# Six stages a batch in place of eight: two columns of 506 or 508 tokens, and w_out's parts reloaded in every stage

## The chip, the cores and the metric

The kernel runs on one core of one Trainium2 chip. The metric is device time in microseconds, the median of several runs. Before the change: 2146.05 us, median of 3 runs (2146.03 to 2146.26).

## The reference

Channel attention followed by two layers of an MLP with squared relu. B = 2, N = 6080 tokens in each batch, C = 256, F = 2048; all float32, the weights float64.

```
qn = q / (norm(q, axis=1) + 1e-6);  kn = k / (norm(k, axis=1) + 1e-6)
a  = softmax(kn^T qn / tau)                 # 256 x 256 for each batch, sums over 6080 tokens
x  = v @ a                                  # [2 * 6080, 256]
x  = (relu(x @ w_in1)^2) @ w_out1           # first layer
out = (relu(x @ w_in2)^2) @ w_out2          # second layer
```

## The kernel before

The program is written in one order by hand (a manual schedule); each engine takes its own instructions from it in that order, and so does SP, which issues all DMAs.

**Attention.** Batch 0's 256 x 256 matrix of scores is made first, from whole tiles, with all engines at it. Its softmax `a` is multiplied into w_in1 (`fuse`, L225, matmuls of 512 columns), so that v needs no matmul of its own. Batch 1's scores are made later, beside the products of batch 0: 24 pieces of 256 tokens. For each piece and each of its two halves `b1_hi` (a cast on ACT), `b1_lo` (a subtraction on DVE), `b1_square` (ACT), `b1_sum` (DVE) and `b1_scores` (six matmuls of 256 columns, L159, into PSUM bank m3) run, and then `b1_add` (DVE, from m3).

**Precision.** Each float32 operand is split into a high and a low float32r part, and a product is three matmuls: high by high, high by low, low by high. The high part is a copy on ACT, the low part a subtraction on DVE.

**Stages, pairs, slots.** The tokens are worked off in stages of two columns of W = 380 tokens: 8 stages for a batch and a layer, 32 in all. In a stage the 16 rows of 128 of F go by pairs: 8 pairs Q. For a pair, h = w_in^T x is made in 7 products of blocks in place of 8 (Winograd's form of Strassen's): `product(Q, k)`, k = 0 to 6, three matmuls each (L806). One product is one slot. Its results go through PSUM banks m0 or m1 (product 3 of the pair before, then 0, 2 and 4), m2 (1 and 5) and m3 (6).

Behind each product `after(Q, k)` issues the elementwise work: the copies u1, u2, u3 out of PSUM, the adds into r (L780), the relu, and for each of the two halves of the pair `square` (on ACT: gh, the high part of the square, L811, and the square itself in r, L812). `lows` (DVE: gl = r - gh) follows one pair later. `relu` goes to ACT or DVE by the table `act_relu`. The y matmuls with w_out (`y_stream`, L870, 24 for a pair, into four banks of their own) run some ten slots behind, 3 or 4 behind each product. At the end of a stage `y_done` copies y out of PSUM and stores it, in the first layer to DRAM (x2d), in the second to the output.

**Background work.** Everything else is put into slots by the table `TIMES` through `at(Q, t, fn)`: slot t after the start of pair Q, a half for behind `after`. So go the right operands of the next stage (`Right`: the load of x, four sums on DVE, seven high parts on ACT, seven low parts on DVE, most of them in the last slots of a stage), the left operands of w_in (`left_steps`), batch 1's pieces (one every two pairs) and its softmax, the first layer's w_out (`conv_task`), and during batch 1 the second layer's weights, whose parts wait in DRAM (wad, wod).

**w_out.** The parts of w_out's eight blocks stay in eight tiles wo0 to wo7 (512 KB each) for a whole layer; `get_out` (L750) loads the second layer's once, in the last stage of the first.

**Tiles.** r0, r1, gh0, gh1, gl0 and gl1 have two buffers each, of 2W words; yo0 and yo1 one of 2W words, stored once a stage.

Of the kernel before, what the change touches and what calls it, by code (L numbers as in the profile page):

```python
# [20 lines left out]
W = 380  # L21
NS = N // (2 * W)
KQ = 7
Y_FIRST = 3
# The order of the work beside the products. Background steps: when they are emitted, in slots (one product each, KQ to a
# pair of rows of f), half a slot for behind the slot's own work. "loads": batch 0's pieces of q and k (p), blocks of weights
# (w) and x; "start": what goes between the pieces and the softmax's steps: the conversion of weights (a, s, m, h, l: as a
# float32 by its steps, its high and its low part) and the first right operands (t: sums, x: high and y: low parts). "rows":
# how many rows of a piece's squares are left to the tensor engine; "act_relu": up to which pair of rows the scalar engine
# does a relu.  # L30
# [21 lines left out]
    "wo": -3,  # L52
    "rows": (1, 1, 1, 1, 1, 2, 1, 1, 1, 1, 1, 2, 1, 1),
    "act_relu": (0, 0, 98, 18),
# [18 lines left out]
def tile_attention_mlp_mlp(  # L73
# [19 lines left out]
    wts = ctx.enter_context(tc.tile_pool(name="wts", bufs=1))  # L93
# [7 lines left out]
    def f32(ap):  # L101
        return ap.bitcast(F32)
# [18 lines left out]
    # A float64 weight as two float32r parts. Its upper word, read as a float32, grows with the weight's size; times 2^16  # L121
    # and held within float32's exponents, its bits shifted by 3 are those of the weight as a float32.
# [192 lines left out]
    with tc.manual_schedule():  # L315
        wa, wo, right = {}, {}, {}
        wop = [ctx.enter_context(tc.tile_pool(name="wop0", bufs=1))]
# [8 lines left out]
        with tc.tile_pool(name="att0", bufs=1) as a0:  # L326
# [76 lines left out]
            # the weights' conversion: one after another, each in steps that the engines' queues take apart  # L403
# [93 lines left out]
            # the first pair of rows' left operands, and what the second's come from, where w_out's last part goes later  # L497
# [16 lines left out]
        wop.append(ctx.enter_context(tc.tile_pool(name="wop1", bufs=1, reuse_waits="tile")))  # L514
# [430 lines left out]
```

## Time and profile before

| | |
|---|---|
| runs | 2146.03, 2146.05, 2146.26 us; median 2146.05 |
| profiled execution, span from first to last instruction | 2140.9 us |
| instructions | 30939 |
| TensorE matmul busy | 2123.4 us (99%), 12264 matmuls |
| DVE busy | 1649.5 us (77%) |
| ACT busy | 1507.8 us (70%) |
| DMA | 128.08 MB, mean 60 GB/s |

The page gives the span of the profiled execution, from its first to its last instruction; its own device time is not listed, and the runs, taken without the profiler, are 5.1 us longer than the span. Busy time of an engine is the union of its instructions' times. Matmuls are pipelined: one is reported as longer than the interval to the next, so the interval between starts, not the reported length, says how fast they go.

### The profile page before, as it was taken

The numbers are of one execution on the slowest core, as the hardware profiler recorded it, in microseconds if no ns is written. First come the engines' busy times: TensorE is split into PE (matmuls) and PEld (weight loads), VectorE is DVE, ScalarE is ACT, GpSimd is POOL, SyncE is SP. The second block draws the span as 40 slices with busy tenths as digits, with TensorE's granted clock in tenths as the row PEclk, the third lists the DMA queues.
The fourth block names the chain that finished last, engine by engine and source line by source line (L and its number), as shares of the span: only waits on it lengthen the run. The fifth ranks groups of instructions, "written<-read, shape, count | busy, mean of one in ns | idle before, by whom it ended". The sixth has DMA issues, their size and how long they took to land.

```text
span 2140.9 us, 30939 instructions
## 1 busy us (share of the span) xinstructions
PE 2123.4 (99%) x12264; PEld 2107.0 (98%) x12264; DVE 1649.5 (77%) x3110; ACT 1507.8 (70%) x2473; POOL 0.7 (0%) x6
## 2 busy tenths in 40 slices
PE   9899999999999999999999999999999999999999
PEld 8799999999999999999999999999999999999999
DVE  7987788878877878788797777777777777777775
ACT  5688778778777777767676666666666666666665
POOL 0000000000000000000000000000000000000000
PEclk9999999999999999999999999999999999999999
DMA  9511111111121212211162000000000000000000
GB/s 347 197 49 45 59 63 66 38 51 57 50 74 45 94 50 76 77 50 69 45 240 100 30 30 30 15 16 30 30 30 30 30 15 16 30 30 30 30 16 15
DMA packets 41857, 128.08 MB, mean 60 GB/s; under 512 B 4784, under 2 KB 5168, under 8 KB 41712
## 3 DMA queue, kind: packets, MB, share of 16 engines
q1 hardware_dynamic: 41712, 126.11, 16.4%
q8 instruction: 96, 1.57, 0.3%
q14 instruction: 49, 0.40, 0.1%
HBM read 85.46 MB, written 40.63 MB: 59 GB/s over the span
## 4 chain that ended last, share of the span: by engine, by line
PE 98%; ACT 1%; DVE 0%; DMA 0%; SPq 0%; issue 0%
PE ps_y L870 50%; PE ps_m L806 43%; PE ps_m L371 2%; PE ps_m L159 2%; PE ps_m L165 1%; PE ps_m L230 0%; PE ps_m L231 0%; PE ps_m L232 0%; DMA araw<-in_q 0%; ACT gh L811 0%; ACT r L812 0%; ACT r L784 0%; SPq L127 0%; DVE x L105 0%; ACT L174 0%
## 5 line engine op out<-in xcount | busy, mean ns | idle before, releaser
L806 PE MATMUL ps_m<-x,wa 128*128 128x380 f32 x5376 | 1221.6, 335 | 6.7 <-DVE u L818 2.2
L870 PE MATMUL ps_y<-gh,wo 128*128 128x380 f32 x4096 | 1164.3, 335 | 0.0
L806 PEld LDWEIGHTS ps_m<-x,wa 128*128 128x128 f32 x5376 | 960.2, 188 | 9.9 <-DVE u L818 2.6
L870 PEld LDWEIGHTS ps_y<-gh,wo 128*128 128x128 f32 x4096 | 746.9, 188 | 0.8
L780 DVE TENSOR_TENSOR r<-u,ps_m 128x380 f32<-128x380 f32 x768 | 421.0, 548 | 398.9 <-PE ps_m L806 208.5
L870 PE MATMUL ps_y<-gl,wo 128*128 128x380 f32 x2048 | 689.3, 337 | 0.0
L811 ACT ACTIVATE gh<-r 128x760 fp32r<-128x760 f32 x512 | 426.3, 833 | 229.1 <-DVE r L786 226.0
L105 DVE TENSOR_TENSOR gl<-r,gh 128x760 fp32r<-128x760 f32 x512 | 483.0, 943 | 6.1 <-ACT r L812 4.8
L812 ACT ACTIVATE r<-r 128x760 f32<-128x760 f32 x512 | 430.5, 841 | 16.3
L870 PEld LDWEIGHTS ps_y<-gl,wo 128*128 128x128 f32 x2048 | 384.6, 188 | 0.5 <-DVE gl L105 0.3
L786 DVE TENSOR_SCALAR r<-r 128x380 f32<-128x380 f32 x652 | 233.3, 358 | 22.4
L836 ACT ACTIVATE r<-ps_m 128x380 f32<-128x380 f32 x256 | 124.8, 488 | 118.2 <-PE ps_m L806 115.9
L832 ACT COPY u<-ps_m 128x380 f32<-128x380 f32 x256 | 122.1, 477 | 106.9 <-PE ps_m L806 105.0
L818 DVE COPY u<-ps_m 128x380 f32<-128x380 f32 x256 | 140.9, 551 | 10.6
L826 ACT COPY u<-ps_m 128x380 f32<-128x380 f32 x256 | 121.3, 474 | 29.8 <-PE ps_m L806 28.3
L784 ACT ACTIVATE r<-r 128x380 f32<-128x380 f32 x116 | 60.5, 522 | 79.9 <-DVE r L780 78.9
L105 DVE TENSOR_TENSOR x<-xt,x 128x380 fp32r<-128x380 f32 x128 | 67.7, 548 | 4.2 <-ACT x L310 1.7
L310 ACT CAST x<-xt 128x380 fp32r<-128x380 f32 x128 | 61.2, 503 | 0.0
L105 DVE TENSOR_TENSOR x<-xraw,x 128x380 fp32r<-128x380 f32 x96 | 52.5, 547 | 0.0
L371 PE MATMUL ps_m<-araw 128*128 128x256 f32 (+1 forms) x192 | 48.0, 402 | 3.4 <-DMA araw<-in_q 3.4
L310 ACT CAST x<-xraw 128x380 fp32r<-128x380 f32 x96 | 48.4, 504 | 0.0
L852 DVE COPY yo<-ps_y 128x380 f32<-128x380 f32 x64 | 35.3, 552 | 13.6 <-PE ps_y L870 13.6
(117 smaller groups left out, 757.1 us busy)
## 6 DMA issues: line engine op xcount, KB each, us to landing
xraw<-in_vT SPq DMA_DIRECT2D x32, 380.0 KB, 3.7
x2d<-yo SPq DMA_DIRECT2D x32, 380.0 KB, 2.3
xraw<-x2d SPq DMA_DIRECT2D x32, 380.0 KB, 3.5
out_T<-yo SPq DMA_DIRECT2D x32, 380.0 KB, 2.3
raw<-in_w_in SPq DMA_DIRECT2D x16, 512.0 KB, 5.0
raw<-in_w_out SPq DMA_DIRECT2D x16, 512.0 KB, 3.9
wad<-unit SPq DMA_DIRECT2D x8, 896.0 KB, 3.6
wa<-wad SPq DMA_DIRECT2D x8, 896.0 KB, 5.4
```

The costliest lines, as they stand in the source:

```text
L105: nc.vector.tensor_tensor(out=out, in0=a, in1=b, op=ALU.subtract)
L310: nc.scalar.copy(self.hi[m], self.operand(m))
L780: nc.vector.tensor_tensor(out=out, in0=a, in1=b, op=op)
L786: nc.vector.tensor_scalar_max(r, r, 0.0)
L806: nc.tensor.matmul(ps, a, b, start=(n == 0 and first), stop=(n == 2), skip_group_check=True)
L811: nc.scalar.square(gh, r)
L812: nc.scalar.square(r, r)
L818: nc.vector.tensor_copy(m["u2"], m[Q, 3])
L826: nc.scalar.copy(u3, m[Q, 3])
L832: nc.scalar.copy(m[Q + 1, "u1"], m[Q + 1, 3])
L836: nc.scalar.activation(m["r", 0][:, 1, :], m[Q, 3], AF.Relu)
L870: nc.tensor.matmul(y[c, n], a, b[:, f, :], start=(p == 0 and f == 0 and x == 0), stop=(p == NQ - 1 and f == 1 and x == 2), skip_group_chec ...
```

## The change

The stages become wider and fewer: the two columns of a stage have 508, 508, 506, 506, 506 and 506 tokens, six stages for a batch and a layer, 24 in all. Each pair has the same matmuls as before, with that many columns.

The wider tiles take the place of w_out in memory. w_out has four tiles in turn in place of eight. In the first stage each block's parts are stored to DRAM once they are made (`stash_out`, w2d), and from the second stage on every stage loads all eight blocks again (`get_out`), each issued at slot 4 of the pair before its own. r and gl have three buffers each for both halves, gh four. gl's tile is taken in `lows` and not in `square`. yo0 and yo1 have one column, and each is stored by itself, two stores for each of them in a stage.

The slots of the background work move. Batch 1's pieces come three in four pairs (`b1_at`) in place of one in two, its softmax is closer packed, and the second layer's weights are converted every 10 pairs in place of 16. `act_relu` counts pairs, and is scaled with their number.

```diff
-W = 380
-NS = N // (2 * W)
+WIDTHS = (508, 508, 506, 506, 506, 506)
+NS = len(WIDTHS)
+W = max(WIDTHS)
+STARTS = [2 * sum(WIDTHS[:i]) for i in range(NS)]
...
-    "wo": -3,
+    "wo": -2,
+    "stash": (0.0, 0.5, 1.0),
+    "get_out": 4.0,
-    "act_relu": (0, 0, 98, 18),
+    "act_relu": (0, 0, 74, 14),
...
-    "b1_hi": (3.0, 5.0),
-    "b1_lo": (4.5, 7.0),
-    "b1_square": (5.0, 9.5),
-    "b1_sum": (9.5, 13.0),
-    "b1_scores": (8.5, 9.0),
-    "b1_add": (9.5,),
-    "b1_soft": (0.0, 2.0, 4.5, 8.0, 9.0, 13.0, 16.5, 16.5, 18.0, 24.0, 24.5),
+    "b1_at": (3.0, 12.5, 22.0),
+    "b1_load": -8.0,
+    "b1_hi": (2.0, 3.5),
+    "b1_lo": (3.0, 4.5),
+    "b1_square": (3.5, 6.0),
+    "b1_sum": (6.0, 8.5),
+    "b1_scores": (5.5, 6.0),
+    "b1_add": (6.5,),
+    "b1_soft": (0.0, 1.5, 3.5, 6.5, 7.0, 9.5, 12.0, 11.5, 12.5, 15.5, 16.5),
...
         def out_tile(n):
-            return wop[n // 4].tile([P, 2, 512], F32R, tag=f"wo{n}", name="wo")
+            return wop.tile([P, 2, 512], F32R, tag=f"wo{n % 4}", name="wo")
...
-            ("w1l", 1024, 1), ("u1", W, 2), ("u2", W, 1), ("u3", W, 1), ("r1", 2 * W, 2), ("r0", 2 * W, 2),
-            ("big", 2048, 1), ("gh1", 2 * W, 2), ("gl1", 2 * W, 2), ("gh0", 2 * W, 2), ("gl0", 2 * W, 2),
-            ("yo0", 2 * W, 1), ("yo1", 2 * W, 1),
+            ("w1l", 1024, 1), ("u1", W, 2), ("u2", W, 1), ("u3", W, 1), ("r", 2 * W, 3), ("big", 2048, 1),
+            ("gh", 2 * W, 4), ("gl", 2 * W, 3), ("yo0", W, 1), ("yo1", W, 1),
...
         for n in range(NP1):
-            Q = NQ + 2 * n
-            at(Q - 2, 2, b1_load, n)
+            Q = NQ + (B1_AT[n % 3] + n // 3 * 4 * KQ) / KQ
+            at(Q, TIMES["b1_load"], b1_load, n)
...
+        def stash_out(n):
+            nc.sync.dma_start(w2d[n], f32(wo[n]))
...
+        UNIT_EVERY = 10
         for j in range(4):
-            Q = Q2 + 2 * NQ * j
+            Q = Q2 + UNIT_EVERY * j
...
-        def get_out(n):
+        def get_out(n, src):
             wo[n] = out_tile(n)
-            nc.sync.dma_start(f32(wo[n]), wod[n])
+            nc.sync.dma_start(f32(wo[n]), src[n])
...
+        for s in range(1, 2 * B * NS):
+            for p in range(NQ):
+                at(s * NQ + p - 1, TIMES["get_out"], get_out, p, w2d if s < B * NS else wod)
...
         def lows(Q, n):
-            gh, gl, r = g[Q, n]
+            gh, r = g[Q, n]
+            gl = g[Q, n][1] = work_tile("gl", r.shape, F32R, 3)
             sub(gl, r, f32(gh))
...
+            yo = work_tile(f"yo{c}", [P, w], F32)
+            (nc.scalar.copy if c else nc.vector.tensor_copy)(yo, y[c, n])
+            o = i // NS * N + STARTS[i % NS]
+            dst = x2d[i][c] if layer == 0 else outT[c * P:(c + 1) * P, o:o + 2 * w]
+            nc.sync.dma_start(dst[:, n * w:(n + 1) * w], yo)
```

How this moves instructions is seen in the order in which each engine has them. In these rows the number in a tile's name tells buffers apart, and the brackets name the engines or DMA queues that a row waits for. TensorE before, at the scores of any of batch 1's pieces (ps_m3 is bank m3, big the piece's parts, x and wa the operands of the products):

```order
L806 MATMUL ps_m2_1768<-x_1431,wa_823 128x380 [waits DVE_49]
L806 MATMUL ps_m2_1768<-x_1432,wa_823 128x380
L806 MATMUL ps_m2_1768<-x_1431,wa_823 128x380
L159 MATMUL ps_m3_1773<-big_1714 128x256 [waits DVE_49]
L159 MATMUL ps_m3_1773<-big_1714 128x256 x5
L870 MATMUL ps_y00_1674<-gh0_1663,wo_632 128x380
L870 MATMUL ps_y10_1691<-gh0_1663,wo_632 128x380
L870 MATMUL ps_y10_1691<-gl0_1664,wo_632 128x380
```

The first six scores stand behind product 1, which is in bank m2. TensorE with the change, at the third piece of a group of three (the sixth of all):

```order
L828 MATMUL ps_m3_2272<-x_1239,wa_1249 128x508
L828 MATMUL ps_m3_2272<-x_1240,wa_1249 128x508
L828 MATMUL ps_m3_2272<-x_1239,wa_1249 128x508
L166 MATMUL ps_m3_2282<-big_2228 128x256 [waits DVE_49,Activation_49]
L166 MATMUL ps_m3_2282<-big_2228 128x256 x5
L893 MATMUL ps_y11_1670<-gl_2203,wo_2048 128x508
L893 MATMUL ps_y11_1670<-gh_2164,wo_2048 128x508
L893 MATMUL ps_y00_1691<-gh_2178,wo_2048 128x508
```

They stand behind product 6 now, which is in the same bank m3. DVE with the change at that place; the wait of TensorE above is for the add that reads ps_m3_2272:

```order
L801 TENSOR_TENSOR r_2215<-u2_2188,ps_m2_2198 128x508 [waits PE_49]
L112 TENSOR_TENSOR big_2228<-raw_2083,big_2228 128x2x256 [waits Activation_49]
L112 TENSOR_TENSOR x_2231<-xt_1684,x_2230 128x506
L801 TENSOR_TENSOR r_2249<-u1_2123,ps_m3_2272 128x508 [waits PE_49]
L807 TENSOR_SCALAR r_2249<-r_2249 128x508 [waits DVE_49]
```

Between the add of product 5 and that of product 6 DVE has the low part of the piece's second half and a step of the right operands. ACT before, around the two casts of a piece (big):

```order
L568 CAST big_3000<-raw_2788 128x2x256 [waits DMAHW7_49,DMAHW0_49]
L832 COPY u1_3002<-ps_m1_2996 128x380 [waits PE_49]
L836 ACTIVATE r0_2986<-ps_m0_2906 128x380 [waits PE_49]
L568 CAST big_3000<-raw_2788 128x2x256
L574 ACTIVATE raw_2788<-raw_2788 128x2x256 [waits DVE_49]
L784 ACTIVATE r1_2987<-r1_2987 128x380 [waits DVE_49]
L811 ACTIVATE gh1_3025<-r1_2987 128x760 [waits Activation_49]
L812 ACTIVATE r1_2987<-r1_2987 128x760 [waits Activation_49]
L811 ACTIVATE gh0_3039<-r0_2986 128x760 [waits DVE_49]
L812 ACTIVATE r0_2986<-r0_2986 128x760 [waits Activation_49]
```

And with the change, at the first piece of a group:

```order
L576 CAST big_2365<-raw_2212 128x2x256 [waits DMAHW2_49,DMAHW1_49]
L805 ACTIVATE r_2325<-r_2325 128x506 [waits DVE_49]
L833 ACTIVATE gh_2369<-r_2325 128x1012 [waits Activation_49]
L834 ACTIVATE r_2325<-r_2325 128x1012 [waits Activation_49]
L833 ACTIVATE gh_2383<-r_2351 128x1012 [waits DVE_49]
L834 ACTIVATE r_2351<-r_2351 128x1012 [waits Activation_49]
L576 CAST big_2365<-raw_2212 128x2x256
L582 ACTIVATE raw_2212<-raw_2212 128x2x256
```

The second cast moved from ahead of the four squares to behind them.

## Rows read from the trace of the kernel before

**Rows 1.** The page's chain of work that ended last, by engine and by line.

```profile
PE 98%; ACT 1%; DVE 0%; DMA 0%; SPq 0%; issue 0%
PE ps_y L870 50%; PE ps_m L806 43%; PE ps_m L371 2%; PE ps_m L159 2%; PE ps_m L165 1%; PE ps_m L230 0%; PE ps_m L231 0%; PE ps_m L232 0%; DMA araw<-in_q 0%; ACT gh L811 0%; ACT r L812 0%; ACT r L784 0%; SPq L127 0%; DVE x L105 0%; ACT L174 0%
```

**Rows 2.** The page's groups: TensorE's matmuls (busy us, mean ns, idle before, releaser).

```profile
L806 PE MATMUL ps_m<-x,wa 128*128 128x380 f32 x5376 | 1221.6, 335 | 6.7 <-DVE u L818 2.2
L870 PE MATMUL ps_y<-gh,wo 128*128 128x380 f32 x4096 | 1164.3, 335 | 0.0
...
L870 PE MATMUL ps_y<-gl,wo 128*128 128x380 f32 x2048 | 689.3, 337 | 0.0
```

**Rows 3.** Busy us (instructions) by stretch: PE, PEld, DVE, ACT, POOL; clock, DMA share, GB/s.

```profile
130.00:550.00 420.00, 420.00 (x2515) 420.00 (x2514) 332.50 (x591) 334.91 (x565) 0.00 (x0) 1.00 0.15 50
1080.00:1120.00 40.00, 40.00 (x233) 40.00 (x232) 37.70 (x79) 29.34 (x52) 0.00 (x0) 1.00 0.81 280
1200.00:2000.00 800.00, 800.00 (x4622) 800.00 (x4621) 584.84 (x1088) 522.43 (x832) 0.00 (x0) 1.00 0.07 26
```

**Rows 4.** Timeline of TensorE at 593 us: six fused matmuls (start us, us, instruction).

```profile
593.76 0.39 PE L230 MATMUL ps_m<-w1h,e 128*128 128x512 f32 x1
593.99 0.40 PE L231 MATMUL ps_m<-w1l,e 128*128 128x512 f32 x1
...
595.15 0.51 PE L870 MATMUL ps_y<-gh,wo 128*128 128x380 f32 x2
```

**Rows 5.** Timeline of TensorE at 329 us: two sets of six scores.

```profile
329.41 0.88 PE L159 MATMUL ps_m<-big 128*128 128x256 f32 x6
330.12 0.51 PE L870 MATMUL ps_y<-gh,wo 128*128 128x380 f32 x2
...
331.16 0.88 PE L159 MATMUL ps_m<-big 128*128 128x256 f32 x6
331.88 0.51 PE L870 MATMUL ps_y<-gh,wo 128*128 128x380 f32 x2
```

**Rows 6.** DMA issues: count, KB each, median us from issue to landing.

```profile
x2d<-yo SPq DMA_DIRECT2D x32, 380.0 KB, 2.3
...
wo<-wod SPq DMA_DIRECT2D x8, 512.0 KB, 3.9
```

**Rows 7.** Groups with shapes kept apart, DVE and ACT.

```profile
L780 DVE TENSOR_TENSOR r<-u,ps_m 128x380 f32<-128x380 f32 x768 | 421.0, 548 | 398.9 <-PE ps_m L806 208.5 <-ACT u L826 188.6
...
L598 DVE TENSOR_TENSOR sacc<-sacc,ps_m 128x512 f32<-128x512 f32 x23 | 15.6, 680 | 0.0
...
L812 ACT ACTIVATE r<-r 128x760 f32<-128x760 f32 x512 | 430.5, 841 | 16.3
L811 ACT ACTIVATE gh<-r 128x760 fp32r<-128x760 f32 x512 | 426.3, 833 | 229.1 <-DVE r L786 226.0
...
L784 ACT ACTIVATE r<-r 128x380 f32<-128x380 f32 x116 | 60.5, 522 | 79.9 <-DVE r L780 78.9
...
L568 ACT CAST big<-raw 128x512 fp32r<-128x512 f32 x48 | 29.6, 616 | 0.0
...
L380 ACT ACTIVATE asq<-araw 128x1024 f32<-128x1024 f32 x1 | 1.1, 1056 | 0.9 <-DMA araw<-in_q 0.9
```

**Rows 8.** Timeline at 157 us: four squares on ACT; a subtraction and the next on DVE.

```profile
157.21 0.84 ACT L811 ACTIVATE gh<-r 128x760 fp32r<-128x760 f32 x1
...
160.43 0.46 ACT L852 COPY yo<-ps_y 128x380 f32<-128x380 f32 x1
...
158.15 0.68 DVE L105 TENSOR_TENSOR big<-raw,big 128x512 fp32r<-128x512 f32 x1
158.75 0.55 DVE L818 COPY u<-ps_m 128x380 f32<-128x380 f32 x1
```

**Rows 9.** Timeline: DVE behind TensorE at 1505 us, TensorE behind DVE at 90 us.

```profile
1505.36 0.68 PE L806 MATMUL ps_m<-x,wa 128*128 128x380 f32 x3
1506.08 0.55 DVE L780 TENSOR_TENSOR r<-u,ps_m 128x380 f32<-128x380 f32 x1 [0.82 <-PE ps_m L806]
...
90.39 0.54 DVE L818 COPY u<-ps_m 128x380 f32<-128x380 f32 x1
...
90.99 0.44 PE L806 MATMUL ps_m<-x,wa 128*128 128x380 f32 x1 [2.24 <-DVE u L818]
```

**Rows 10.** The chain in order of time, at the start of the products.

```profile
74.21 1.39 DVE x L105 x3
```

More of the change, by code (lines that the diff above doesn't have):

```diff
@@ L20 @@
 NQ = F // P // 2
-W = 380
-NS = N // (2 * W)
+WIDTHS = (508, 508, 506, 506, 506, 506)
+NS = len(WIDTHS)
+W = max(WIDTHS)
+STARTS = [2 * sum(WIDTHS[:i]) for i in range(NS)]
+assert 2 * sum(WIDTHS) == N
 KQ = 7
@@ L243, in left_tile @@
     def left_tile(p):
-        return wts.tile([P, 2, KQ, P], F32R, tag=f"wa{p}", name="wa")
+        return wts[p // 4].tile([P, 2, KQ, P], F32R, tag=f"wa{p}", name="wa")
     def left_steps(dst, wf, r, sums):
@@ L272, in left_steps @@
         return sums1, hi1, sums2, lo1, hi2, lo2
-    x2d = [dram.tile([CC, P, 2 * W], F32, name=f"x2d{i}") for i in range(B * NS)]
+    x2d = [dram.tile([CC, P, 2 * WIDTHS[i % NS]], F32, name=f"x2d{i}") for i in range(B * NS)]
     class Right:
@@ L290, in x @@
         def x(self, c, n):
-            return self.raw[:, c, n * W:(n + 1) * W]
+            return self.raw[:, c, n * self.w:(n + 1) * self.w]
         def sums(self, n):
             if n == 0:
-                self.t = [xp.tile([P, W], F32, tag=f"xt{i}", name="xt") for i in range(4)]
+                self.t = [xp.tile([P, self.w], F32, tag=f"xt{i}", name="xt") for i in range(4)]
             t, x = self.t, self.x
@@ L307, in split_hi @@
             self.hi[m], self.lo[m] = [
-                xp.tile([P, W], F32R, tag=f"x{t}{m}", name="x", bufs=1 if m < 4 else 2) for t in "hl"
+                xp.tile([P, self.w], F32R, tag=f"x{t}{m}", name="x", bufs=1 if m < 4 else 2) for t in "hl"
             ]
@@ L554, in tile_attention_mlp_mlp @@
         NP1 = -(-N // (2 * P))
+        B1_AT = TIMES["b1_at"]
         def b1_load(n):
@@ L681, in tile_attention_mlp_mlp @@
             fused_tasks(NQ * NS + 2 * j - 4, 1, j)
-        for n in range(len(wo), NQ):
+        w2d = [dram.tile([P, 2, 512], F32, name=f"w2d{p}") for p in range(NQ)]
+        def stash_out(n):
+            nc.sync.dma_start(w2d[n], f32(wo[n]))
+        for n in range(NQ):
+            if n in wo:
+                at(0, TIMES["stash"][n], stash_out, n)
+                continue
             def wo_hi(n=n):
@@ L801, in product @@
             if first:
-                m[Q, k] = bank({1: "m2", 3: a, 6: "m3"}[k])[:, 0:W]
+                m[Q, k] = bank({1: "m2", 3: a, 6: "m3"}[k])[:, 0:xr.w]
             ps = m[Q, {0: 3, 1: 1, 2: 3, 3: 3, 4: 3, 5: 1, 6: 6}[k]]
@@ L822, in after @@
             elif k == 2:
-                for n in range(2):
-                    m["r", n] = work_tile(f"r{n}", [P, 2, W], F32, 2)
-                u3 = work_tile("u3", [P, W], F32)
+                m["r", 1] = work_tile("r", [P, 2, w], F32, 3)
+                u3 = work_tile("u3", [P, w], F32)
                 nc.scalar.copy(u3, m[Q, 3])
@@ L844, in after @@
                 square(Q, 0)
-        y, yo = {}, {}
+        y = {}
         def y_done(s, c, n):
             layer, i = divmod(s, B * NS)
-            if n == 1:
-                yo[c] = work_tile(f"yo{c}", [P, 2 * W], F32)
-            (nc.scalar.copy if c else nc.vector.tensor_copy)(yo[c][:, n * W:(n + 1) * W], y[c, n])
-            if n == 0:
-                dst = x2d[i][c] if layer == 0 else outT[c * P:(c + 1) * P, i * 2 * W:(i + 1) * 2 * W]
-                nc.sync.dma_start(dst, yo[c])
+            w = WIDTHS[i % NS]
+            yo = work_tile(f"yo{c}", [P, w], F32)
[3 more added lines that the diff above has]
+            nc.sync.dma_start(dst[:, n * w:(n + 1) * w], yo)
         def y_stream():
@@ L861, in y_stream @@
                 for n in (1, 0):
-                    gh, gl, _ = g[Q, n]
+                    gh, gl = g[Q, n]
                     for c in range(CC):
                         if p == 0:
-                            y[c, n] = bank(f"y{c}{n}")[:, 0:W]
+                            y[c, n] = bank(f"y{c}{n}")[:, 0:right[s].w]
                         for f in range(2):
```

25 lines of the change are left out of this document (14 added, 11 removed).

## The prediction

> **What bounds the kernel now.** I read the page's chain of waits first: TensorE carries 98% of what ended last, half in w_out's matmuls, 43% in w_in's products [rows 1]. So the time is TensorE's count of matmuls times the interval between two starts, plus what it waits. The groups give the count: 5376 + 4096 + 2048 = 11520 matmuls of 380 columns [rows 2]. The busy time by stretch gives the interval: 4622 of them start in 800 us from 1200 us on, 173.1 ns each, with TensorE busy all the time at full clock [rows 3]. 130 to 550 us, in which batch 1's scores are computed beside the products, has no idle time either. DVE is busy 79% there and ACT 80% (332.50 and 334.91 of 420 us), so neither is a bound, but both are close enough that the order of their instructions counts. Transfers slow nothing: from 1080 to 1120 us the DMA engines were 81% busy, and TensorE still started 233 matmuls in 40 us [rows 3].
>
> The profiled execution has a span of 2140.9 us; the median of the runs, 2146.05 us, is 5.1 us more, for what lies around the span. I take these 5.1 us as unchanged and count differences from 2146.05. No change means within 0.2%, 4.3 us: 2141.8 to 2150.3.
>
> **1. Fewer, longer matmuls.** 24 stages in place of 32, 360 matmuls in each: 8640 in place of 11520. Columns stay the same in sum (11520 x 380 = 8640 x 506.67). What is saved is what a matmul costs beside its columns. The trace has two other widths. Six fused matmuls of 512 columns go from 593.76 to 595.15 us, 231.7 ns each [rows 4]. Two sets of six score matmuls of 256 columns take 0.71 and 0.72 us, 119.2 ns each [rows 5]. The line through 256 and 380 gives 228.2 ns at 506.67 columns, the line through 380 and 512 gives 229.3. I take 228.8: 8640 x 228.8 = 1976.8 us against 11520 x 173.1 = 1994.1 us, **-17.3 us** (-22.5 to -12.9).
>
> The Trainium skill (TensorE: Matmul & The Clock Gate, Back-to-back issue gap) puts a warm interval at N/2.4 + 2.5 ns. That is 160.8 ns for 380 columns; this trace shows 173.1, so here it does not hold, and by it the saving would be 2880 x 2.5 = 7.2 us.
>
> **2. w_out reloaded.** There are 184 loads of 512 KB (8 in each of 23 stages) in place of 8, and 8 stores of the parts in the first stage. A load of this kind landed 3.9 us after its issue [rows 6]. It may be issued when the matmuls of four pairs earlier have read the tile, in slot 2 of the pair two before its own; it is needed in slot 3 of the pair behind its own: three pairs of some 10.3 us. What stands ahead of it on SP (batch 1's loads, the stores of y, x) waits for work of earlier slots. I cost it at nothing; if a load did come late, TensorE would wait at the first y matmul of that pair. The traffic, 4 MB in about 82 us, is some 51 GB/s, far below the 280 GB/s beside which no matmul was slower [rows 3].
>
> **3. Batch 1's scores at three places.** Before, a piece's scores always stood after products 1 and 2 of a pair. Now three pieces share four pairs, and they stand at three places. All three write bank m3, which product 6 of each pair uses too.
>
> Durations for the new width, from the groups [rows 7]: an add on DVE 0.68 us (548 ns at 380 columns, 680 at 512); a square on ACT 1.05 us (833 and 841 at 760, 1056 at 1024); relu or cast of 508 columns 0.63 us (522 at 380, 616 at 512). Back to back they overlap a little: a 0.68 us subtraction on DVE was followed 0.60 us after its start; four squares started within 157.21 to 160.43 us, 0.805 us apart [rows 8], so 1.02 apart now. From PE's end to a waiting DVE passes 0.04 us (1505.36 + 0.68 to 1506.08), from DVE's end to a waiting PE 0.06 (90.39 + 0.54 to 90.99) [rows 9]. A 512-column matmul is reported as 0.39 to 0.40 us from start to end [rows 4].
>
> *Third piece.* Its first scores follow product 6 on TensorE directly and wait for DVE's add that reads product 6 from m3. Count from the end of product 5: DVE starts that product's add at 0.04, then a score operand's low part, then a step of the right operands, each holding the queue 0.60; product 6's add starts at 1.84, ends at 2.52, and TensorE goes on at 2.58. TensorE itself is there after 4 y matmuls and product 6: 8 x 0.229 - 0.395 = 1.44. It idles **1.14 us**, in 8 pieces **9.1 us**. At the least, with DVE free when product 6 ends, it is 0.395 + 0.04 + 0.68 + 0.06 - 0.229 = 0.95 us, 7.6 in all; with no overlap on DVE 1.4 us, 11.
>
> *First piece.* ACT's copy of its second half now stands behind the pair's four squares; before, it stood ahead of them. From the end of product 5: add 0.04 + 0.68, relu 0.06 + 0.66, squares 4.07, copy 0.61, so 6.12; DVE's low part is ready for TensorE at 6.92. TensorE arrives after 26 matmuls and six scores, and needs it one score later: 27 x 0.229 + 7 x 0.119 - 0.395 = 6.62. **0.3 us**, eight times 2.4.
>
> *Second piece.* The copies stand behind the squares too, and the low part behind u3, the add and a relu; the same count comes to a wait of about **0.2 us**, eight times 1.6. These two are small differences of long chains: nothing at the least, 0.6 us a piece at the most (9.6 us), if one cast more lies on the chain.
>
> Sum for part 3: 9.1 + 4.0 = **+13.1 us** (7.6 to 20.6).
>
> **4. Start.** Batch 0's softmax is a chain through all engines. Three low parts on it took 1.39 us [rows 10]; each of them is 0.13 longer, as are two or three more operand steps in front, and the first two copies are 0.1 longer each: **+1.2 us** (0 to 2.5). The first pairs, without y beside them, follow DVE and ACT, whose steps grow by some 25%; the matmuls there grow by 32% and are in part 1.
>
> **5. Small ones.** One half of batch 1's softmax now reads m3 in slot 5, right ahead of product 6: +0.5. y is stored by halves from one tile each, so the copy of the second half waits for the first's store. A store landed after 2.3 us [rows 6]; twelve matmuls, 2.75 us, lie between, and beside products it is longer. Only at the very end may this show: +0.3. The second layer's weights are converted every 10 pairs (102 us) in place of 16 (125 us), with more time per slot: nothing. Three tiles for r and gl each in place of four: the reader of the tile is done three slots before it is written: nothing. Sum **+0.8**.
>
> **The sum.** 2146.05 - 17.3 + 13.1 + 1.2 + 0.8 = 2143.9, say **2144.0 us**: no change that can be told. With the ends of its own terms nearby, 2139 to 2149.
>
> **Rivals.**
> *Faster: the new waits stay at their least.* Only product 6's read of m3 is certain, since TensorE cannot pass it. If ACT and DVE are early everywhere else: 2146.05 - 17.3 + 7.6 + 1.2 + 0.8 = 2138.4, and 2133 with 228.2 ns a matmul. For it: before, TensorE never waited between 130 and 550 us [rows 3]. Against: there the copies stood ahead of the squares. Chance 0.25.
> *Slower: ACT falls behind in the stretch of the scores.* One cast more (0.63 us) ahead of the copies of the sixteen first and second pieces: 2143.9 + 16 x 0.63 = 2154. It is slower than 2150.3 as soon as each of the sixteen waits 0.4 us longer than counted. For it: ACT is 80% busy there, and casts of right operands stand in the second half of every stage. Against: most of those stand elsewhere. Chance 0.16.
> *Slower: the interval grows with the columns,* and a longer matmul saves nothing: 173.1 x 506.67 / 380 = 230.8 ns, 8640 of them again 1994 us, and 2146.05 + 13.1 + 1.2 + 0.8 = 2161. Against: in proportion 256 columns would take 116.6 ns and 512 would take 233.2; the rows have 119.2 and 231.7 [rows 4, 5]. Chance 0.04. The Trainium skill's page named above lies between the two: by its 2.5 ns the time would be 2146.05 - 7.2 + 15.1 = 2154.0.
> That the change doesn't do what it says is excluded: TensorE's order has 8640 matmuls of 506 or 508 columns.
>
> **How the numbers follow.** The forecast has 0.55. Faster by over 0.2%: the first rival and the lower 3 us of the forecast's ten, 0.25 + 0.28 x 0.55 = 0.40. Slower: the other two, 0.20. Within: 0.40. The range goes from 2133, the first rival's end, to 2154, the second one's value; some 0.17 lie outside, mostly above.
>
> **What would show it.** Right: an interval of 228 to 229.5 ns in an undisturbed stretch of the second layer; TensorE idle by 7 to 14 us in some 8 large waits for DVE's add into r and up to 16 small ones for the score operands, all before 550 us; none for wo's loads. Wrong: an interval over 230 or below 227.5; no wait ahead of the scores; waits for wo, or a stretch after 700 us with TensorE idle.

## The result and the profile after

The change takes **2163.39 us** (median of 4 runs, 2160.16 to 2164.7) where the kernel before took 2146.16 (4 runs): ratio 1.0082, 95% interval 1.0068 to 1.0097. It is 17.2 us slower; the forecast was 2144.0, with a range up to 2154.

The page of the kernel after: its span, the chain by line, TensorE's groups and the reloads (columns as in [rows 1, 2, 6]).

```profile
span 2162.9 us, 24661 instructions
...
PE 91%; DVE 5%; ACT 2%; DMA 1%; issue 0%; SPq 0%; ACTq 0%; DVEq 0%
PE ps_y L893 47%; PE ps_m L828 41%; PE ps_m L166 2%; DVE r L801 1%; ACT gh L833 1%; ACT r L834 1%; DVE asq L395 1%; DMA wod<-wo_parts 1%; DVE x L112 0%; DVE big L112 0%; PE ps_m L237 0%; PE ps_m L239 0%; PE ps_m L238 0%; DMA raw<-in_w_in 0%; DVE conv L141 0%
...
L828 PE MATMUL ps_m<-x,wa 128*128 128x506 f32 (+1 forms) x4032 | 1150.1, 394 | 11.8 <-DVE u L841 4.4
L893 PE MATMUL ps_y<-gh,wo 128*128 128x506 f32 (+1 forms) x3072 | 1051.3, 393 | 0.0
...
L893 PE MATMUL ps_y<-gl,wo 128*128 128x506 f32 (+1 forms) x1536 | 602.7, 392 | 0.0
...
L166 PE MATMUL ps_m<-big 128*128 128x256 f32 x288 | 45.2, 289 | 8.6 <-DVE r L801 8.3
...
wo<-wod SPq DMA_DIRECT2D x96, 512.0 KB, 3.5
wo<-w2d SPq DMA_DIRECT2D x88, 512.0 KB, 4.6
```

There are 4032 + 3072 + 1536 = 8640 long matmuls, as said, and no wait for `wo`. But TensorE's share of the chain fell from 98% [rows 1] to 91%: DVE, ACT and a store (`wod<-wo_parts`) stand on it now. By stretch:

```profile
130.00:550.00 420.00, 411.37 (x1894) 336.19 (x1893) 317.58 (x476) 309.99 (x446) 0.00 (x0) 1.00 0.28 95
1080.00:1120.00 40.00, 35.44 (x141) 27.98 (x140) 27.39 (x46) 22.27 (x32) 0.00 (x0) 0.91 0.75 267
1200.00:2000.00 800.00, 800.00 (x3478) 655.35 (x3477) 557.50 (x823) 496.80 (x630) 0.00 (x0) 1.00 0.22 74
```

Against [rows 3], the first two stretches have idle time that was not there, and in the third a matmul takes 800 / 3478 = 230.0 ns. A stage there lasts 82.85 us (mean of stages 12 to 22, from the start of a stage's first long matmul to that of the next stage's), where it was 62.35 before; 24 of them are 1988.4 us against 32, 1995.2.

**The third piece's scores** follow product 6 and wait for DVE's sum. The timeline of TensorE at 260 us (start, us, instruction):

```profile
260.00 0.85 PE L828 MATMUL ps_m<-x,wa 128*128 128x508 f32 x3
261.90 0.95 PE L166 MATMUL ps_m<-big 128*128 128x256 f32 x6 [1.04 <-DVE r L801]
```

The 1.04 us is reckoned from the reported end; from start to start the last product and the scores are 1.42 to 1.45 us apart in eight places, 1.2 us over an interval. From start to start too, a first piece waits 0.3 us and a second one 0.1 us. With these, and some 3 us of small waits of products, stages 1 to 4 hold 16.0 us beyond their matmuls.

**Stage 11**, with the first of the left operands' loads (get_left), takes 90.9 us. The waits of 1085 to 1107 us (who, for whom, us in total, times, longest), and the end of the chain there in order of time (start, us, what):

```profile
DVE sums L258 <- DMA wod<-wo_parts: 4.9, 1, 4.9
...
PE ps_m L828 <- DVE r L801: 3.1, 1, 3.1
ACT unit L262 <- DMA wad<-unit: 2.4, 1, 2.4
...
DVE xt L112 <- DMA xraw<-x2d: 1.9, 1, 1.9
...
PE ps_m L828 <- DVE u L841: 1.3, 1, 1.3
```

```profile
1085.63 0.71 DVE wo_parts L112
...
1086.36 11.23 DMA wod<-wo_parts
...
1097.61 0.30 DVE sums L258
...
1099.17 0.60 DVE r L801
...
1099.82 0.79 PE ps_m L828
```

Tile w1l serves first w_out's parts, then the next unit's sums (wo_begin, unit_begin). The store that frees it took 11.2 us. At that time the queues carried 373 GB/s: this store, the unit's, x, y, the reloads and the left operands (896 KB each). DVE stands for 4.9 us, behind it in its queue the adds that TensorE waits for.

```profile
1099.00:1106.00 7.00, 6.18 (x15) 4.94 (x16) 5.12 (x9) 2.77 (x4) 0.00 (x0) 0.51 0.27 61
1082.00:1098.00 16.00, 13.26 (x56) 9.94 (x54) 8.40 (x15) 8.42 (x14) 0.00 (x0) 1.00 1.01 373
```

After the idle time the granted clock is 0.51, the 1.2 GHz level, for seven us: 15 matmuls in place of some 30.

The kernel before also stored its last units beside these loads, and its TensorE never waited there [rows 3]. SP's queue before:

```profile
1082.66 1.08 SPq L855 DMA_DIRECT2D x2d<-yo  x2
...
1094.24 0.32 SPq L748 DMA_DIRECT2D wa<-wad  x1
1094.97 0.32 SPq L712 DMA_DIRECT2D wad<-unit  x1
1101.54 0.32 SPq L718 DMA_DIRECT2D wod<-wo_parts  x1
```

That store of wo_parts landed after 3.0 us. The loads of x and y's stores had been issued more than 11 us ahead of the unit's store. With the change two loads of x, the unit's store, two stores of y, a reload and the store of wo_parts are issued within four us, from 1082.43 to 1086.36 us.

**Batch 1's softmax** (stage 5) is the fourth place, from the waits of TensorE and of DVE from 558 to 600 us:

```profile
PE ps_m L828 <- DVE u L841: 1.8, 1, 1.8
...
DVE d L214 <- ACT s L209: 1.7, 1, 1.7
```

DVE's step ahead of the reciprocal (d) waits for an exponential that ACT does behind four squares; u2 stands behind it on DVE. Here too the granted clock falls behind the wait: 0.83 in the mean from 578 to 588 us.

### The profile page after: what moved, and what is told of

Its sections match the earlier page's. It is cut to its first block, busy times and chain, and to the rows that moved or that the text cites. A ratio compares the mean times of both kernels' runs of the same rounds, so it can differ in the third digit from the quotient of the medians.

```text
span 2162.9 us, 24661 instructions
## 1 busy us (share of the span) xinstructions
PE 2131.9 (99%) x9384; PEld 1744.6 (81%) x9384; DVE 1575.2 (73%) x2458; ACT 1427.5 (66%) x1925; POOL 0.7 (0%) x6
## 4 chain that ended last, share of the span: by engine, by line
PE 91%; DVE 5%; ACT 2%; DMA 1%; issue 0%; SPq 0%; ACTq 0%; DVEq 0%
PE ps_y L893 47%; PE ps_m L828 41%; PE ps_m L166 2%; DVE r L801 1%; ACT gh L833 1%; ACT r L834 1%; DVE asq L395 1%; DMA wod<-wo_parts 1%; DVE x L112 0%; DVE big L112 0%; PE ps_m L237 0%; PE ps_m L239 0%; PE ps_m L238 0%; DMA raw<-in_w_in 0%; DVE conv L141 0%
## 5 line engine op out<-in xcount | busy, mean ns | idle before, releaser
L828 PE MATMUL ps_m<-x,wa 128*128 128x506 f32 (+1 forms) x4032 | 1150.1, 394 | 11.8 <-DVE u L841 4.4
L893 PE MATMUL ps_y<-gh,wo 128*128 128x506 f32 (+1 forms) x3072 | 1051.3, 393 | 0.0
L828 PEld LDWEIGHTS ps_m<-x,wa 128*128 128x128 f32 x4032 | 761.1, 189 | 188.1 <-DVE u L841 6.0
L801 DVE TENSOR_TENSOR r<-u,ps_m 128x506 f32<-128x506 f32 (+1 forms) x576 | 392.2, 681 | 429.0 <-PE ps_m L828 251.3
L893 PE MATMUL ps_y<-gl,wo 128*128 128x506 f32 (+1 forms) x1536 | 602.7, 392 | 0.0
L833 ACT ACTIVATE gh<-r 128x1012 fp32r<-128x1012 f32 (+1 forms) x384 | 400.8, 1044 | 220.0 <-DVE r L807 217.6
L112 DVE TENSOR_TENSOR gl<-r,gh 128x1012 fp32r<-128x1012 f32 (+1 forms) x384 | 463.3, 1207 | 3.5 <-ACT r L834 3.5
L834 ACT ACTIVATE r<-r 128x1012 f32<-128x1012 f32 (+1 forms) x384 | 404.1, 1052 | 12.2
L807 DVE TENSOR_SCALAR r<-r 128x506 f32<-128x506 f32 (+1 forms) x488 | 207.5, 425 | 16.9
L854 ACT COPY u<-ps_m 128x506 f32<-128x506 f32 (+1 forms) x192 | 112.0, 584 | 121.0 <-PE ps_m L828 121.0
L848 ACT COPY u<-ps_m 128x506 f32<-128x506 f32 (+1 forms) x192 | 111.4, 580 | 81.2 <-PE ps_m L828 77.6
```

The lines of the kernel that those rows point to most:

```text
L112: nc.vector.tensor_tensor(out=out, in0=a, in1=b, op=ALU.subtract)
L801: nc.vector.tensor_tensor(out=out, in0=a, in1=b, op=op)
L807: nc.vector.tensor_scalar_max(r, r, 0.0)
L828: nc.tensor.matmul(ps, a, b, start=(n == 0 and first), stop=(n == 2), skip_group_check=True)
L833: nc.scalar.square(gh, r)
L834: nc.scalar.square(r, r)
```

## The account

Between the two profiled executions, us:

| part | forecast | found |
|---|---|---|
| long matmuls, whole stages | -17.3 | 1988.4 - 1995.2 = -6.8 |
| scores, stages 1 to 4 | +13.1 | 16.0 + 0.2 = +16.2 |
| start (first product at 77.91, was 76.43) and stage 0 | +1.2 | +1.5 - 0.7 = +0.8 |
| softmax, stage 5 | +0.5 | 5.3 - 1.4 = +3.9 |
| stage 11 | 0 | +8.0 |
| end | +0.3 | 0 |
| sum | -2.2 | +22.1 |

The spans differ by 2162.9 - 2140.9 = 22.0. The medians differ by 17.2, because the profiled execution of before was a short one: every later run is about 1.8 us longer than its span, so it took 2142.7, 3.4 under its median, while the one after took 2164.7, 1.3 above. The 5.1 us that the prediction put around the span were 1.8 of this kind and 3.3 that only this execution was short.

One profile each doesn't settle the row of the start. In the profiled executions of the change and of five runs below that have its widths (without reload, and those that move the work), the first product starts between 77.46 and 79.90 us, and the granted clock of the first 90 us is between 0.89 and 0.98. That spread is larger than the row's 0.8 us.

## The experiments

Intervals with two decimals are the distance between the starts of a matmul in a stage's third pair of rows and the 240th behind it, divided by 240. A window's count takes in one or two matmuls that only reach into it. Ratios are to the kernel before.

**Is it the reload?** In stages 1 on, y takes `wo[4 + p % 4]`, and get_out isn't issued. This leaves out half of the first layer's w_out and all of the second's; the count of matmuls is the same.

```diff
-        for s in range(1, 2 * B * NS):
+        for s in range(0):
...
-                w = wo[p]
+                w = wo[p] if s == 0 else wo[4 + p % 4]
```

> w_out's parts aren't loaded again: stages 1 to 23 use the four pairs of rows that stage 0 left in the rotating tiles, so this run leaves out half of w_out and all of the second layer's. Everything else stands as in the change. Theory A (a matmul's interval is a fixed part plus a part per column, 230.1 ns at 508 columns whatever the DMA queues do): stages 13 to 22 stay at 82.85 us each, and only the stretch at 1090 to 1106 us can gain, where the reloads share the queues with the left operands' loads: 2157 to 2163 us. Theory B (the reload's traffic, 74 GB/s where it was 26, stretches the matmuls from the forecast's 228.8 to 230.1 ns): a stage falls to 82.4 us, 24 of them give back 11 us, with the stretch at 1090 us 2146 to 2152.

2160.8 us (1.006 to 1.009). The window of 1200 to 2000 us without reload:

```profile
1200.00:2000.00 800.00, 800.00 (x3478) 655.38 (x3477) 558.31 (x824) 495.70 (x631) 0.00 (x0) 1.00 0.08 25
```

The same 3478 matmuls, beside 25 GB/s in place of 74; every stage from 12 on lasts the same to 0.01 us. The traffic costs a matmul nothing: theory B falls. Stage 11 went to 87.3 us, 3.5 less. Only 0.9 of this are shorter waits of TensorE (1.7, 1.6 and 0.4 us in place of 3.1, 1.3 and 0.2). The rest is the clock, which stayed at full speed in this execution:

```profile
1099.00:1106.00 7.00, 6.70 (x29) 5.50 (x30) 6.86 (x12) 4.02 (x5) 0.00 (x0) 1.00 0.42 88
```

In stage 5 it did so as well, behind the same wait of 1.8 us as in the change (granted clock 1.00 in the ten us behind it, where the change has 0.83). So the reload's share of the 8 us is 0.9 to 3.5: that the clock stayed up because the reload was gone is not shown.

**The width alone undone, and one between.**

```diff
-WIDTHS = (508, 508, 506, 506, 506, 506)
+WIDTHS = (380,) * 8
...
-    "act_relu": (0, 0, 74, 14),
+    "act_relu": (0, 0, 98, 18),
```

(`act_relu` counts pairs, and has its old values for eight stages.) And in between, with `act_relu` as in the change:

```diff
-WIDTHS = (508, 508, 506, 506, 506, 506)
+WIDTHS = (436,) + (434,) * 6
```

> The change with eight stages of 380 columns again: the reload, the four rotating tiles and the new order of the background work stay, the width alone is undone. Theory A: a stage without background work takes 62.35 us as in the kernel before (173.2 ns a matmul), and the time is that of before plus the waits of the new order (scores 16, softmax 4, start 1; the left operands' loads no longer meet the last units): 2163 to 2170. Theory B (traffic): a stage takes over 62.7 us, 32 of them 11 us more: 2175 to 2181.

> The change with seven stages of 436 or 434 columns. Theory A, a line through 173.2 ns at 380 and 230.1 at 507 (0.449 ns a column and 2.5 ns beside): 197.6 ns a matmul, 71.1 us a stage. If the interval grew in proportion to the columns, 197.9 ns and 71.25 us; if the forecast's 0.440 ns a column held up to here and something else begins between 434 and 508 columns, 197.1 ns and 70.95 us. Time by theory A: 28 x 71.1 = 1991 against 1995 for the stream, and 21 of waits and start: 2160 to 2166.

380 columns: 2190.86 us (1.020 to 1.023), 172.7 to 173.0 ns. Interval as theory A said, time over 20 us above it: three pieces in four pairs of rows are now three in 31 us, not 41, while DVE's and ACT's chains for a piece are as long as before; stages 1 to 4 have 29 us of waits. The new order of the background work needs the long stages; that the chains are the reason is argued from their lengths. 434 columns: 2185.26 us (1.017 to 1.020), again some 20 us above what was expected, with 22 us of waits in stages 1 to 4. The interval is 197.8 to 198.4 ns, above the line through the other two.

**The order of the work.** Third piece later; units closer; softmax later; then all three, with the casts a slot earlier.

```diff
-    "b1_at": (3.0, 12.5, 22.0),
+    "b1_at": (3.0, 12.5, 23.5),
```
```diff
-        UNIT_EVERY = 10
+        UNIT_EVERY = 8
```
```diff
-    "b1_soft": (0.0, 1.5, 3.5, 6.5, 7.0, 9.5, 12.0, 11.5, 12.5, 15.5, 16.5),
+    "b1_soft": (0.0, 1.5, 4.0, 8.0, 9.5, 11.0, 13.0, 11.5, 12.5, 15.5, 16.5),
```
```diff
-    "b1_hi": (2.0, 3.5),
-    "b1_lo": (3.0, 4.5),
+    "b1_hi": (1.0, 2.5),
+    "b1_lo": (2.5, 4.0),
```

> The change with the third piece's steps 1.5 slots later, so that its scores stand behind product 0 or 1 and not behind product 6, whose sum DVE still has to read from the bank. If that wait (eight of 1.2 us in the trace) is the path, 9.6 us less than the change: 2152 to 2155, and no gap of 1.4 us from a product to the scores in stages 1 to 4. Rival: the squares that stand ahead of the casts are the next wait, and the third piece then waits for its casts as the first does: 0.3 us a time is back, 2 to 3 us, 2155 to 2158. Against both: if TensorE only waits elsewhere for the same work of DVE, the time stays at 2163.

2157.08 us, 6.3 less: the rival's time, but not its mechanism. Stages 1 to 4 go from 381.6 to 374.2 us. The waits that TensorE's rows of scores have now are those for the casts and low parts:

```profile
PE ps_m L166 <- DVE big L112: 1.0, 3, 0.3
PE ps_m L166 <- ACT big L576: 1.0, 3, 0.3
```

They aren't the third piece's, which no longer waits at all. They are three of the eight first pieces', whose second cast stands behind the four squares. One of them, at the start of stage 2:

```profile
278.01 0.38 PE L166 MATMUL ps_m<-big 128*128 128x256 f32 x1 [0.35 <-ACT big L576]
278.73 0.50 PE L166 MATMUL ps_m<-big 128*128 128x256 f32 x2 [0.34 <-DVE big L112]
```

From start to start these three wait 1.2 us each in place of 0.3, and the first wait in batch 1's softmax is 0.9 us longer: 9.6 less 2.7 less 0.9 is 6.0, about the 6.3 measured.

> The change with the second layer's four units of weights every 8 pairs of rows and not every 10: the last is stored some 8 pairs earlier, before the left operands are loaded back in stage 11. If it is the meeting of these loads with the unit's stores and the reload that stalls the queues (a store of wo_parts 11.2 us from issue to landing, with DVE and then TensorE behind it), stage 11 falls from 90.9 to about 83.5 us and the time to 2155 to 2157. Rival: the left operands' loads and the reload fill the queues by themselves, and another transfer (x for the next stage) is late: 2 to 4 us stay, 2158 to 2161.

2155.15 us, 8.2 less. Stage 11 takes 82.82 us, and the two windows of above hold

```profile
1082.00:1098.00 16.00, 16.00 (x71) 13.11 (x70) 10.78 (x16) 9.89 (x12) 0.00 (x0) 1.00 0.77 283
1099.00:1106.00 7.00, 7.00 (x32) 5.72 (x31) 4.95 (x8) 3.17 (x5) 0.00 (x0) 1.00 0.12 36
```

no idle time and full clock, at 283 GB/s, with get_left and the reload still there. Moving the last units away removes all of stage 11's 8 us: it was their meeting with the other transfers.

> The change with the exponentials of batch 1's softmax and the steps behind them 1.5 slots later, away from the four squares. If DVE's reciprocal, which waits for the exponential behind the squares and holds up u2 behind it, is what costs there (0.9 and 2 us of TensorE idle, then four us at half clock), 3 to 4 us less: 2159 to 2161. Rival: the transposes now come later beside product 6, which waits for the bank: 0.5 to 1 us comes back, 2160 to 2162. If the half clock comes from something else, 1 to 2 us less.

2161.79 us (2160.04 to 2163.47): 1.6 less, within the spread of the runs. In the profiles stage 5 went from 97.95 to 94.49 us, but it was 96.4 in two other runs that left it alone (without reload, and units closer): there the waits were the same, but the clock stayed at full speed. So 1.9 us are sure.

> The last three edits in one, and the casts of every piece of batch 1 a slot earlier, ahead of the squares. If the waits add up, 9.6 + 8 + 3.5 + about 3 of small waits less than the change: 2139 to 2143, under the kernel before by 3 to 7 us, which is the stream's 6.8 us less the start's 1.2. If the waits only give way to one another, 2146 or more.

**2143.09 us** (11 runs; 0.9981 to 0.9999). The waits add up, at the upper end of what was expected: 20.3 us less than the change. With the casts a slot earlier no first piece waits any more. Stages 1 to 4 keep 4.6 us of waits, stage 5 1.8, stage 11 none. That is 2.3 us under the kernel before: the 6.8 us of the long matmuls, less the waits that are left.

**What sets the interval?** Only WIDTHS is changed in the next runs, in the second of them beside the four edits of the order.

```diff
-WIDTHS = (508, 508, 506, 506, 506, 506)
+WIDTHS = (508, 508, 508, 508, 504, 504)
+WIDTHS = (508, 508, 508, 508, 504, 504)
+WIDTHS = (512, 512, 504, 504, 504, 504)
+WIDTHS = (510, 510, 506, 506, 506, 502)
```

> The change with stages of 508, 508, 508, 508, 504 and 504 columns: the same sum, every width a multiple of four. In the change the stages of 506 columns took 230.1 ns a matmul, those of 508 229.9, and 434 took 198.1, more than a line between 380 and 508 gives (197.3). Theory C (a matmul takes the time of the next multiple of four columns, 0.445 ns for each): 508 columns 229.9 ns, 504 columns 228.1, 229.3 in the mean against 230.06, and 8640 x 0.76 = 6.6 us less: 2156 to 2158. Theory A as it stood (a line, with tiles' places worth a few tenths of a ns): the mean width is the same, so 2162 to 2164. If the multiple is eight, 504 columns take 226.3 to 226.5 ns and the time falls by 11 us.

> The widths of 508 and 504 with all edits of the order (third piece's scores 1.5 slots later, casts a slot earlier, units every 8 pairs, softmax later): 2143.1 for these edits with the old widths, less 6.6 by theory C: 2136 to 2138, under the kernel before by 8 to 10 us. By theory A: 2142 to 2144.

> The change with stages of 512, 512, 504, 504, 504 and 504 columns. Theory C: 231.7 ns (the fused matmul of 512 columns) and 228.1, 229.3 in the mean, as with 508 and 504: 2156 to 2158. Theory A: 2162 to 2164. If eight is the multiple: 231.7 and 226.4 to 228.1.

> The change with stages of 510, 510, 506, 506, 506 and 502 columns, no width a multiple of four. Theory C: 510 takes what 512 takes (231.7 ns), 506 what 508 takes (229.9 to 230.1), 502 what 504 takes (228.1): 230.2 in the mean, 0.2 over the change, 2163 to 2166. Theory A with 0.445 ns a column from 229.9 at 508: 230.8, 229.0 and 227.2, 229.3 in the mean and 2155 to 2158.

2155.26 us (1.0033 to 1.0061), with the edits 2136.19 (0.9944 to 0.9971), within 1 us of what theory C had: 229.85 and 228.1 ns. The next two refuted it. 512 columns: 2151.74 us (1.0017 to 1.004); the windows inside stages 12 and 13 (512 columns) and 14 to 17 (504):

```profile
1180.00:1310.00 130.00, 130.00 (x575) 107.70 (x574) 91.62 (x136) 83.20 (x105) 0.00 (x0) 1.00 0.20 65
1340.00:1640.00 300.00, 300.00 (x1312) 247.16 (x1311) 207.54 (x309) 185.70 (x237) 0.00 (x0) 1.00 0.23 72
```

The longer matmuls are the faster ones: 226.67 ns against 229.05. And 506 columns, 230.1 in the change, took 228.8 in the last of the four (2158.91 us, one run).

Are some lengths free of a cost? The second again has the four edits.

```diff
-WIDTHS = (508, 508, 506, 506, 506, 506)
+WIDTHS = (512, 512, 512, 512, 512, 480)
+WIDTHS = (512, 512, 512, 512, 512, 480)
+WIDTHS = (512, 512, 512, 508, 500, 496)
+WIDTHS = (384,) * 7 + (352,)
```

(the last with `act_relu` at its old values again)

> The change with stages of 512, 512, 512, 512, 512 and 480 columns. Theory D (a length that is a multiple of 16 or 32 columns takes 0.443 ns a column with nothing beside it, every other length some 4.5 ns more): 226.7 and 212.6 ns, 224.4 in the mean, 8640 x 5.7 = 49 us less than the change: 2112 to 2117. Theory E (only 512 columns, where the tiles' halves lie 2 KB apart, are free of it): 226.7 and 217 ns, 225.1 in the mean, 43 us less: 2118 to 2123. Theory A, a line over the columns: 2162 to 2164.

> The same widths with all edits of the order (third piece's scores later, casts earlier, units every 8 pairs, softmax later; 2143.1 us at the old widths). If the two gains add up: 2092 to 2101. If shorter matmuls let DVE and ACT become the bound in stages 0 to 5, 5 to 10 us of it stay out: 2101 to 2110.

> The change with stages of 512, 512, 512, 508, 500 and 496 columns. Theory D with 16 as the multiple: 496 columns take 219.7 ns, 500 and 508 226.3 and 229.9. With 32 as the multiple, or by theory E: 496 columns take 224.5. The time follows the stages: 2137 to 2144.

> The change with eight stages again, of 384 (seven) and 352 columns; the nearest run is the one with 380 columns, 172.9 ns and 2190.9 us. Theory D: 170.0 and 155.9 ns, 168.3 in the mean, so that short matmuls cost no more per column than long ones; 8 to 10 us less in each eight stages where TensorE alone sets the pace (16 to 24 of 32): 2150 to 2165. Theory E: 174.7 and 160.4 ns, 172.9 in the mean: 2188 to 2193.

2129.34 us (0.9911 to 0.9938): 34 less than the change, 9 short of theory E's 43. 512 columns take 226.67 again (81.60 us a stage, 1.25 less than in the change), 480 take 217.6 (78.55, 4.3 less): 20 x 1.25 + 4 x 4.3 = 42 us where TensorE sets the pace alone. But stages 1 to 4 gave 0.9 of their 5.0, since waits for DVE and ACT set theirs. With the edits: **2103.64 us** (0.9793 to 0.982), 41 us below the kernel before, within what the rival said. Its windows:

```profile
130.00:550.00 420.00, 416.65 (x1965) 347.63 (x1964) 330.86 (x494) 319.30 (x458) 0.00 (x0) 1.00 0.29 96
1080.00:1120.00 40.00, 40.00 (x185) 34.44 (x185) 27.91 (x45) 26.82 (x36) 0.00 (x0) 1.00 0.41 146
1250.00:1500.00 250.00, 250.00 (x1105) 207.01 (x1104) 177.75 (x262) 159.54 (x200) 0.00 (x0) 1.00 0.23 76
```

496 columns took 223.3 (2133.78 us, one run, 3 us below what was expected), so 16 isn't the multiple; 384 took 173.33 and 352 160.8 (2180.2 us, 1.0149 to 1.0177, between the two forecasts), so neither theory's 170.0 or 174.7. The window with 384 columns:

```profile
1700.00:2050.00 350.00, 350.00 (x2021) 350.00 (x2020) 258.32 (x479) 229.95 (x367) 0.00 (x0) 1.00 0.28 91
```

384 and 512 columns (to 0.03 ns in every stage whose neighbours have the same length) lie 53.34 ns apart for 128 columns: 0.4167 ns each, one column a cycle at the 2.4 GHz level. With that slope both have 13.3 ns beside it, less than any other length has. Against 13.3 + 0.4167 N (N is the number of columns) every other length has an extra:

| columns | ns | extra | | columns | ns | extra |
|---|---|---|---|---|---|---|
| 352 | 160.8 | 0.8 | | 500 | 224.9 | 3.2 |
| 380 (before) | 173.25 | 1.6 | | 504 | 228.1, 229.05 | 4.7, 5.7 |
| 384 | 173.33 | 0 | | 506 (change) | 230.1 | 6.0 |
| 434 | 198.1 | 4.0 | | 506 (with 510) | 228.8 | 4.6 |
| 480 | 217.6 | 4.2 | | 508 (change) | 229.9 | 4.9 |
| 496 | 223.3 | 3.3 | | 508 (with 500) | 228.7 | 3.7 |
| 510 | 229.9 | 4.1 | | 512 | 226.67 | 0 |

Two last runs asked what the extra hangs on: tiles padded to 512 words, and a multiple of 64.

```diff
-    gl = g[Q, n][1] = work_tile("gl", r.shape, F32R, 3)
+    gl = g[Q, n][1] = work_tile("gl", [P, 2, 512], F32R, 3)[:, :, 0:r.shape[2]]
...
-            gh = work_tile("gh", r.shape, F32R, 4)
+            gh = work_tile("gh", [P, 2, 512], F32R, 4)[:, :, 0:r.shape[2]]
```

(the right operands' tiles likewise)

> The change with its widths of 508 and 506, but every tile that TensorE streams (right operands, high and low parts of the squares) 512 words apart, so that all of them and their second halves begin at a multiple of 32 bytes; what is computed is the same. Theory F1 (the extra hangs on where a stream begins: in the run with 508 and 500 columns, streams of 508 took 227.9 ns from a multiple of 32 bytes and 230.4 from 16 behind one): 227 to 228 ns, 8640 x 2.0 to 3.0, 18 to 26 us less than the change: 2137 to 2146. Theory F2 (the length alone): 230.06 ns and 2162 to 2164.

> The change with seven stages, five of 448 and two of 400 columns. By 13.3 ns and 0.4167 a column: 200.0 and 180.0 ns where a length is free of the extra. If multiples of 64 are: 200.0 in every stage of 448. If only multiples of 128 are: 201 to 204. 400 columns: 181 to 184.

Padded: 2169.45 us (1.0095 to 1.0129), 230.6 to 230.9 ns, so F1 falls: the extra got larger, not smaller. F2 isn't right either, since the same lengths took 230.06 before. 448 columns took 202.67 ns in most stages, 2.7 over 200.0, and 400 took 182.0 to 182.5 (2172.52 us, one run): a multiple of 64 is not free.

The run with 448 columns shows something more. From 680 us, behind the fused matmuls in stage 7, up to the next wait, at the start of stage 9, each interval is 206 or 207 ns, 206.67 in the mean. Behind that wait they run through some 199, 207, 203, 202 and 203 ns, over and over, whichever tiles are read: 202.67 in the mean. Windows in stage 8, in a stretch of it without any transfer, and in stage 15:

```profile
745.00:805.00 60.00, 60.00 (x292) 54.50 (x291) 48.60 (x86) 44.53 (x70) 0.00 (x0) 1.00 0.50 168
797.00:801.00 4.00, 4.00 (x21) 3.63 (x20) 3.82 (x8) 3.97 (x8) 0.00 (x0) 1.00 0.00 0
1250.00:1310.00 60.00, 60.00 (x298) 55.60 (x297) 41.52 (x69) 39.22 (x56) 0.00 (x0) 1.00 0.28 89
```

So one length in one kernel has two steady intervals, and it changed from one to the other at a wait. At 512 and at 384 columns there was one level: in undisturbed stages between stages of the same length every interval is 226 or 227 ns, or 173 or 174. At 506 they scatter from 221 to 241 ns. What the extra hangs on stays open, but it isn't the length alone.

## Why the prediction was wrong

**Step 1, the long matmuls, failed** (10.5 us of the miss), at its line: "The line through 256 and 380 gives 228.2 ns at 506.67 columns, the line through 380 and 512 gives 229.3." No line through these rows holds. The rows of 512 columns that it rested on, six fused matmuls at 231.7 ns [rows 4], aren't what 512 columns take in a long stream, 226.67. The idea of the step was right and larger than thought: 2880 matmuls fewer at 13.3 ns are 38 us. But the widths chosen give most of it back, by an extra at 506 and 508 columns that no row of the trace before showed. The extra is 1.6 ns at 380 columns (11520 x 1.6 = 18 us) and 5.6 on average at 508 and 506 (8640 x 5.6 = 48 us): 18 + 38 - 48 = 8 us less, 6.8 over whole stages.

The rival by which the interval grows with the columns gave 2161, nearest to the result, with 0.04. That was luck: it had no gain where 6.8 us were found, and 15.1 us of waits and start where 28.9 were found. Its mechanism is excluded, since in proportion 512 columns would take 233 ns. The Trainium skill (TensorE: Matmul & The Clock Gate, Back-to-back issue gap) gives N/2.4 + 2.5 ns for the gap of an isolated matmul, not for a stream with weight loads as here. The traces agree with its column part (53.34 ns for 128) and not with the other (13.3); the 7.2 us that it gave came near the 6.8 for another reason.

**Step 5 failed** (11 us): "The second layer's weights are converted every 10 pairs [...] nothing." (Ten pairs at its 228.8 ns are 103 us, not 102; nothing hangs on that.) It counted the time per slot of the conversion and not what the last unit's stores meet: they now fall together with x's loads and y's stores of pair 89, in which get_left starts too. The 8.0 us came from there, shown by moving the units. **Step 2** said nothing for the reload, and in an undisturbed stage that is right to 0.01 us; it had left out that one stage in which other loads already fill the queues, although that place of the kernel before stood in [rows 3] (81% of the DMA engines, at 1080 us). The reload has 0.9 to 3.5 of the 8 us. Of the softmax, step 5 looked at product 6 and not at the exponential behind the squares: 3.9 us in place of 0.5. Both prices include half clock behind a wait, for which the sum had no term.

**Step 3, the scores, was right in its mechanism:** 8 x 1.2 us for the third piece (9.1 forecast), 8 x 0.3 for the first (2.4 forecast), 8 x 0.1 for the second (1.6 forecast). The 16.2 in place of 13.1 comes from some 3 us of small waits of products, which it didn't count. The rival for ACT wasn't met: no cast more stood on the chain. **Step 4** gave 1.2, and 0.8 was found, within the spread of the start between executions: neither confirmed nor refuted.

"What would show it" had named both failures under "Wrong": an interval over 230, and TensorE idle after 700 us.

## What to carry to other kernels

Take the price of a matmul's length from a long stream of that very length, and where none is in the trace, run it, in the kernel itself: here 4 columns (508 or 512) were worth more than 128 (380 or 508), and 506 took 230.1 ns in one kernel and 228.8 in another. A schedule kept in slots is stretched or squeezed by a change of the slot: look again for steps that now stand behind a bank's reader or a run of squares, and for the first and last of each series of transfers, where two series meet.

## What the runs showed of the hardware

At full clock a float32r matmul in a stream with a weight load each took 13.3 ns and 0.4167 a column at 384 and 512 columns. All other lengths took 0.8 to 6.7 ns more. This differed by 1.4 ns for one length (506) between two kernels, by 4 ns for one length (448) in one kernel, from one wait to the next, and it was not less when the streamed tiles were padded to 512 words. At 506 and 508 columns it made no difference whether DMA moved 25 or 74 GB/s beside the stream.

A stall of some three us on TensorE was followed by about seven us at half clock (1099 to 1106 us): of the 8 us that stage 11 lost, some 3.5 (15 matmuls fewer at 0.23) lie there. The clock doesn't always fall: the same wait of 1.8 us in stage 5 was followed by half clock in the change (0.83 in the mean of the ten us behind it) and by full clock in two other runs (1.00). One 512 KB store took 11.2 us where the queues carried 373 GB/s, against a median of 2.9 for its kind.
